# Attention and a gated feed-forward in one kernel: bfloat16 score corrections, v by a DMA transpose, weights ahead of the keys, one reciprocal per tile, a new order

## The chip, the cores and the metric

The kernel runs on one core of one Trainium2 chip. Its time is the device time of one execution, in microseconds (us), median of several runs. TensorE (PE in the profile) multiplies matrices, VectorE (DVE) and ScalarE (ACT) work on SBUF and PSUM, GpSimd (POOL) on SBUF alone, and SyncE (SP) issues every DMA of this kernel. Each engine works through its own list in order and waits on semaphores for the others.

## The reference

Four batches; q has 12288 rows of 128. The keys, which are also the values, are means of kv over windows of 4 x 4, 768 rows of 128 per batch, times a 128 x 128 matrix. The attention's output goes into a feed-forward with a squared ReLU and a sigmoid gate, in which each row is mixed with the row before it.

```python
kv_pool = kv.reshape(B, H // r, r, W // r, r, C).mean(axis=(2, 4))
k = v = kv_pool.reshape(B, -1, C) @ w_sr
s = (q @ k.transpose(0, 2, 1)) / np.sqrt(C)
a = np.exp(s - s.max(-1, keepdims=True))
a /= a.sum(-1, keepdims=True) + 1e-09
x = a @ v
x_prev = x shifted by one row
xk = mu_k * x + (1.0 - mu_k) * x_prev          # xr in the same way with mu_r
k = np.maximum(xk @ w_k, 0.0)                   # 128 -> 1024
out = 1.0 / (1.0 + np.exp(-(xr @ w_r))) * (k * k @ w_v)
```

Everything is float32. The kernel gets there with narrower products by splitting: an operand is rounded to a high part, the rest is a low part, and high x low, low x high and high x high are added in PSUM.

## The kernel before

The host hands over q transposed (`qT`), the kv windows with channels on partitions (`kv0` for the first batch, `kvw` for the others) and the three feed-forward weights as 64-bit words, two 32-bit halves each, which the kernel converts into pairs of 16-bit matrices (`wkh`, `wkl`, `wvh`, `wvl`, `wvb`, `wrh`, `wrl`).

**A tile** is 512 rows of q; there are 24 per batch, 96 in all. Its steps, with the names of the code:

- `qf` loads, `qh` (ScalarE) rounds to fp32r, `ql` (POOL) is the rest.
- `S0` to `S3`: the scores of 128 rows each against 768 keys, in chunks of 512 and 256 columns. A *score group* is the six products of one `S`: `ql` x `ksh`, `qh` x `ksl`, `qh` x `ksh` in each chunk, all fp32r.
- `nm` (VectorE): the negated row maximum. `ex` (ScalarE): the exponential, with the row sum in `sm`. Its result `pe` is in SBUF for three groups; the fourth, `S3`, is overwritten in PSUM and stays there.
- `rc` (VectorE): two tiny instructions, 1/(sum) for two groups at a time. `f1` (ScalarE): the normalised fp16 part of `pp`. `f2` (VectorE, `pp<-pe,rc,pp`): its fp16 rest.
- `tt`: one DMA transpose per group, of both parts, into `pT`.
- `AV0` to `AV5` (`px<-pT,v`): 18 products with the fp16 parts `v1`, `v2` of v. `xe`, `xk`, `xr`: the mixing; `xkh`, `xkl`, `xrh`, `xrl`: the split.
- `ha`, `hb` (`ph`): 24 products for the hidden layer in four quarters; `r`, `k2`, `kh`, `kl`: ReLU, square and split, spread over ScalarE, VectorE and POOL; `va`, `vb` (`pv`): 24 products back. `z` (`pz`): 3 products for the gate; `th`, `T1`, `E`, `E1`, `g`, `o`, and `so` stores.

**Buffers.** A `Ring` hands out its buffers in turn, so a step that takes one waits for the last reader of what was in it. Scores and `ph` share the ring `big` of three PSUM buffers; `px`, `pz` and the key preparation share `x`, which has one. Key loads have six (`kv`), `pT` two.

**Once and per batch.** For the first batch the keys come in twelve loads of 512 KB: eight (`kva`) for keys 0 to 511, multiplied straight away in fp32 (`pk`), and four (`kvb`) summed on VectorE first (`four`). The weights are loaded (`raw`) and converted into 16 bits in steps whose names begin with `w`: about nine VectorE instructions for each 512 columns, an absolute-sum product with `ones` (`cs`) and a maximum for a common scale. For the later batches twelve key loads with a VectorE sum each (`br`, `acc<-kvt`) are spread over twelve tiles, and about a tile's time later comes `PREP`: `pk`, `ks`, `am`, `ex`, the split `ksh`, `ksl`, and v: `ksv` scales, `pt0` and `pt1` transpose on PE in fp32, `v1*` and `v2*` copy and split. `dg` with `ones` (in `pt1`) spreads a maximum over partitions; `sv` and `uz` are scales.

**Order.** The code writes no loop order. Each step is put on a heap with a number and taken off in the order of the numbers:

```python
def plan_tile(i, b, t):
    if i < len(EARLY):            places, base = EARLY[i], 0.0
    elif i >= NTILES - len(LATE): places, base = LATE[...], i * PERIOD
    else:                         places, base = WHEN, i * PERIOD
    def at(name):
        def put(fn): plan.add(places[name] + base, name, fn, ("tile", i))
```

`WHEN` is for the middle, `EARLY` for the first tiles (six lists), `LATE` for the last four, `ONCE` for the steps before the first scores and the weights, `PREP` for later batches. The numbers set only who stands before whom in each engine's list. Every instruction is recorded under one line of a helper (L37), so in the profile tiles tell the steps apart.

Of the kernel before, what the change touches and what calls it, by code (L numbers as in the profile page):

```python
# [23 lines left out]
K_SHIFT = 23  # L24

# [46 lines left out]
def tile_kernel(ctx, tc, qT, kv0, kvw, w_sr, mu_k, mu_r, w_k, w_v, w_r, outT):  # L72
# [20 lines left out]
    ones = const.tile([P, P], F32, name="ones")  # L93
    nc.vector.memset(ones, 1.0)
    wsr = const.tile([P, C], F32, name="wsr")
    nc.sync.dma_start(out=wsr, in_=w_sr)
# [8 lines left out]
    mu = const.tile([P, 2], F32, name="mu")  # L105
    mix = const.tile([P, 4], F32, name="mix")
    mtop = const.tile([P, 2], F32, name="mtop")
    cz = const.tile([P, 3], F32, name="cz")
# [3 lines left out]
    for name, shape, dtype in (  # L112
        ("qf", [P, T], F32), ("qh", [P, T], F32R), ("ql", [P, T], F32R),
        ("pe", [P, K], F32), ("sm", [P, NSUB], F32), ("rc", [P, NSUB], F32), ("nm", [P, 1], F32),
        ("pp", [P, 2, K], F16), ("pT", [P, NSUB, 2 * NK, P], F16),
        ("xek", [P, T + 1], F32), ("xer", [P, T + 1], F32), ("xk", [P, T], F32), ("xr", [P, T], F32),
        ("xkh", [P, T], F16), ("xkl", [P, T], F16), ("xrh", [P, T], F16), ("xrl", [P, T], F16),
        ("E", [P, T], F32), ("th", [P, T], F32), ("o", [P, T], F32),
        ("rr", [P, 2 * T], F32), ("kk", [P, 2 * T], F32), ("kh", [P, 2 * T], F16),
        ("kl", [P, 2 * T], BF16), ("kv", [P, 1024], F32),  # L120
        ("ksh", [P, K], F32R), ("ksl", [P, K], F32R), ("v1", [P, NK, P], F16), ("v2", [P, NK, P], F16),
        ("s4", [P, 4], F32), ("uz", [P, 3], F32), ("sc", [P, 1], F32),
        ("ks", [P, K], F32), ("acc", [P, K], F32), ("dg", [P, 2, P], F32),
    ):
        rings[name] = Ring(sb, name, shape, dtype, BUFS.get(name, 2))
# [24 lines left out]
    @once("L_mu")  # L150
    def _():
        for i, src in enumerate((mu_k, mu_r)):
            sp.dma_start(out=mu[:, i:i + 1], in_=src.rearrange("(p o) -> p o", o=1))

# [16 lines left out]
    def weights(name, w, hi, lo, half, extra):  # L171
        st = {}
        n = w.shape[1]
        least = 897.0 if half else 896.0
        parts = [(c, min(n, c + 512)) for c in range(0, n, 512)]
        top, rest = {}, {}

        def part(i, c0, c1):
# [8 lines left out]
            @once(f"we_{key}")  # L187
            def _():
                st["e", i] = take("xk", name="e", dtype=I32)[:, :d]
                dve.tensor_scalar(  # L190
                    st["e", i], st["raw", i][:, :, 1], 20, 0x7FF,
                    op0=ALU.logical_shift_right, op1=ALU.bitwise_and,
                )
# [37 lines left out]
            def _():  # L231
                if "top" not in st:
                    st["top"] = take("kk", name="top")
                st["t", i] = st["top"][:, c0:c1]
                dve.tensor_tensor(
                    out=st["t", i].bitcast(I32), in0=st["m", i], in1=st["ei", i], op=ALU.bitwise_or
# [3 lines left out]
            def _():  # L240
                if "rest" not in st:
                    st["rest"] = take("rr", name="rest")
# [6 lines left out]
            def _():  # L249
                st["a", i] = take("o", name="wabs")[:, :d]  # L250
# [26 lines left out]
        for i, (c0, c1) in enumerate(parts):  # L277
# [20 lines left out]
            if extra is not None:  # L298
                @once(f"wb_{name}{i}")
# [20 lines left out]
    def first_keys(ks, ksh, ksl):  # L320
        st = {"a": 0, "b": 0}
        for i in range(WIN // 2):
            @once(f"L_a{i}")
            def _(i=i):
                st[f"a{i}"] = take("kv", name="kva", shape=[P, 2, 512])
                sp.dma_start(out=st[f"a{i}"], in_=kv0[:, 2 * i:2 * i + 2, 0:512])

            @once(f"pa{i}")
            def _(i=i):
                if st["a"] == 0:  # L330
                    st["pk"] = take("big", name="pk")
# [7 lines left out]
        for i in range(WIN // 4):  # L339
            @once(f"L_b{i}")  # L340
            def _(i=i):
                st[f"b{i}"] = take("kv", name="kvb", shape=[P, 4, K - 512])
                sp.dma_start(out=st[f"b{i}"], in_=kv0[:, 4 * i:4 * i + 4, 512:K])

            @once(f"ab{i}")
            def _(i=i):
                st[f"s{i}"] = take("xek", name="four", shape=[P, K - 512])
                dve.tensor_reduce(
                    out=st[f"s{i}"], in_=st[f"b{i}"].rearrange("p w k -> p k w"), axis=AX.X,
                    op=ALU.add,  # L350
                )

            @once(f"pb{i}")
            def _(i=i):
                if st["b"] == 0:
                    st["pk2"] = take("big", name="pk")
                pe.matmul(
                    st["pk2"][:, 0:K - 512], lhsT=wsr, rhs=st[f"s{i}"],
                    start=(st["b"] == 0), stop=(st["b"] == WIN // 4 - 1),
                )  # L360
                st["b"] += 1

        for n, (c0, c1) in enumerate(CHUNKS):
# [12 lines left out]
            def _(c0=c0, c1=c1):
                dve.tensor_tensor(
                    out=ksl[:, c0:c1], in0=ks[:, c0:c1], in1=ksh[:, c0:c1].bitcast(F32),
                    op=ALU.subtract,
                )  # L380

    def later_keys(b, i0, at, ks, ksh, ksl):
        st = {}

        def part(n):
# [30 lines left out]
        @at("ksh")  # L416
        def _():
            dve.tensor_copy(out=ksh, in_=ks)

        @at("ksl")  # L420
        def _():
            pool.tensor_tensor(out=ksl, in0=ks, in1=ksh.bitcast(F32), op=ALU.subtract)

    def batch_prep(b, i0, res):
# [10 lines left out]
        ks, ksh, ksl = take("ks"), take("ksh"), take("ksl")  # L435
        (later_keys if later else first_keys)(*((b, i0, at) if later else ()), ks, ksh, ksl)
        v1, v2, s4, uz, sc = (take(n) for n in ("v1", "v2", "s4", "uz", "sc"))
# [3 lines left out]
        res += [ksh, ksl, v1, v2, s4, uz, sc]  # L441
        st = {}
# [11 lines left out]

        @at("dg")
# [7 lines left out]
        @at("ksv")  # L463
        def _():
            st["ksv"] = take("acc", name="ksv")
            dve.tensor_scalar_mul(st["ksv"], ks, ivs)

        for h, (j0, j1) in enumerate(((0, 4), (4, NK))):
            @at(f"pt{h}")
            def _(h=h, j0=j0, j1=j1):  # L470
                pt = st["pt", h] = take("x", name="pt", shape=[P, 4, P])
# [30 lines left out]
        def _():  # L502
            dve.tensor_scalar_mul(uz, cz, xt[:, 1:2])
            dve.tensor_scalar(sc, cv, xt[:, 0:1], xt[:, 0:1], op0=ALU.mult, op1=ALU.mult)

    def plan_tile(i, b, t):
        st = {}
        if i < len(EARLY):
# [594 lines left out]
```

## Time and profile before

| | us |
|---|---|
| timed runs: median (lowest to highest) of 3 | 1919.85 (1918.26 to 1920.95) |
| profiled execution, span from first to last instruction | 1917.4 |
| what the median has beside that span | 2.45 |
| granted PE clock, mean | 0.995 |
| PE / VectorE / ScalarE / POOL busy | 1881.0 / 1754.2 / 1699.9 / 1069.0 |

In rows of groups the columns are: line, engine, operation, out<-in, shapes, count, then busy us and mean ns, then the idle time before and what ended it. An fp32 product is recorded as two. PE's records overlap, since products are pipelined: what one costs is the distance from its start to the next start, and not its length. A window row gives the stretch, then busy us and instructions of PE, weight loads (PEld), VectorE, ScalarE and POOL, then PE's clock, the busy share of the DMA engines and GB/s.

### The profile page before, as it was taken

The numbers are of one execution on the slowest core, as the hardware profiler recorded it, in microseconds if no ns is written. First come the engines' busy times: TensorE is split into PE (matmuls) and PEld (weight loads), VectorE is DVE, ScalarE is ACT, GpSimd is POOL, SyncE is SP. The second block draws the span as 40 slices with busy tenths as digits, with TensorE's granted clock in tenths as the row PEclk, the third lists the DMA queues.
The fourth block names the chain that finished last, engine by engine and source line by source line (L and its number), as shares of the span: only waits on it lengthen the run. The fifth ranks groups of instructions, "written<-read, shape, count | busy, mean of one in ns | idle before, by whom it ended". The sixth has DMA issues, their size and how long they took to land.

```text
span 1917.4 us, 26966 instructions
## 1 busy us (share of the span) xinstructions
PE 1881.0 (98%) x9022; PEld 1033.4 (54%) x9022; DVE 1754.2 (91%) x2582; ACT 1699.9 (89%) x2432; POOL 1069.0 (56%) x784
## 2 busy tenths in 40 slices
PE   7699999999999999999999999999999999999999
PEld 4355555555555555555555555555555555555554
DVE  5999999998999999999999999999898989898898
ACT  3699998899898989889999999988999999999997
POOL 1265555556565656556555555555555555555556
PEclk9899999999999999999999999999999999999999
DMA  6556564546566666446566656554646464655452
GB/s 224 117 127 141 135 146 97 105 108 116 116 141 136 139 136 130 99 104 117 103 140 130 146 132 144 111 110 97 124 97 124 97 124 96 124 98 123 83 118 59
DMA packets 640523, 230.57 MB, mean 120 GB/s; under 512 B 606336, under 2 KB 608640, under 8 KB 640384
## 3 DMA queue, kind: packets, MB, share of 16 engines
q1 hardware_dynamic: 640384, 228.85, 56.0%
q8 instruction: 71, 1.16, 0.3%
q14 instruction: 68, 0.56, 0.1%
HBM read 52.63 MB, written 25.17 MB: 41 GB/s over the span
## 4 chain that ended last, share of the span: by engine, by line
PE 94%; DVE 3%; ACT 1%; DMA 1%; issue 1%; SPq 0%; DVEq 0%
PE pv L37 26%; PE ph L37 25%; PE S L37 20%; PE px L37 19%; PE pz L37 3%; DVE pp L37 1%; DVE nm L37 1%; PE pk L37 0%; DMA kva<-kv 0%; DMA kvb<-kv 0%; ACT pp L37 0%; PE pt L37 0%; DVE top L37 0%; ACT rr L37 0%; SPq L37 0%
## 5 line engine op out<-in xcount | busy, mean ns | idle before, releaser
L37 POOL TENSOR_TENSOR kl<-kk,kh 128x1024 bf16<-128x1024 f32 x288 | 653.8, 2271 | 240.5 <-ACT kh L37 226.2
L37 ACT ACTIVATE rr<-ph 128x1024 f32<-128x1024 f32 x384 | 392.8, 1024 | 46.1 <-PE ph L37 40.1
L37 DVE TENSOR_REDUCE nm<-S 128x1 f32<-128x768 f32 x384 | 364.8, 952 | 66.4 <-PE S L37 59.3
L37 PE MATMUL px<-pT,v 128*128 128x512 f16 x1728 | 421.8, 380 | 3.3 <-DVE xr L37 2.9
L37 POOL TENSOR_TENSOR xrl<-xr,xrh 128x512 f16<-128x512 f32 x96 | 146.3, 1524 | 326.6 <-DVE xrh L37 326.6
L37 PE MATMUL S<-ksh,ql 128*128 128x512 f32 (+1 forms) x768 | 299.0, 389 | 8.9 <-ACT pe L37 4.7
L37 ACT ACTIVATE kh<-rr 128x1024 f16<-128x1024 f32 x288 | 302.7, 1052 | 2.3 <-PE pv L37 1.7
L37 DVE SCALAR_TENSOR_TENSOR pp<-pe,rc,pp 128x768 f16<-128x768 f32 x288 | 292.3, 1037 | 1.8 <-ACT pp L37 1.7
L37 PE MATMUL ph<-xkh,wkl 128*128 128x512 f16 x768 | 291.1, 379 | 2.2 <-ACT pe L37 2.2
L37 ACT ACTIVATE pp<-pe,rc 128x768 f16<-128x768 f32 x288 | 260.3, 938 | 36.5 <-DVE rc L37 32.1
L37 PE MATMUL pv<-kh,wvl 128*128 128x512 f16 x768 | 292.0, 380 | 0.0
L37 PE MATMUL pv<-kh,wvh 128*128 128x512 f16 x768 | 291.1, 379 | 0.0
L37 PE MATMUL ph<-xkh,wkh 128*128 128x512 f16 x768 | 291.1, 379 | 0.0
L37 PEld LDWEIGHTS <-v 128*128 128x128 f16 x1728 | 169.3, 98 | 209.2 <-issue 6.1
L37 DVE TENSOR_TENSOR kk<-ph,rr 128x1024 f32<-128x1024 f32 x192 | 234.7, 1223 | 48.6 <-ACT rr L37 48.5
L37 ACT ACTIVATE pe<-S,nm 128x768 f32<-128x768 f32 x288 | 258.7, 908 | 11.2 <-DVE nm L37 9.8
L37 PE MATMUL S<-ksl,qh 128*128 128x512 f32 (+1 forms) x768 | 260.9, 340 | 0.2 <-ACT ks L37 0.2
L37 PE MATMUL S<-ksh,qh 128*128 128x512 f32 (+1 forms) x768 | 260.9, 340 | 0.0
L37 PEld LDWEIGHTS <-wkh 128*128 128x128 f16 x1536 | 150.3, 98 | 183.6 <-issue 3.4
L37 PE MATMUL ph<-xkl,wkh 128*128 128x512 f16 x768 | 228.1, 379 | 0.0
L37 POOL TENSOR_TENSOR xkl<-xk,xkh 128x512 f16<-128x512 f32 x96 | 113.7, 1184 | 198.8 <-DVE rc L37 180.9
L37 PE MATMUL pv<-kl,wvb 128*128 128x512 bf16 x768 | 213.2, 379 | 0.0
(120 smaller groups left out, 2811.4 us busy)
## 6 DMA issues: line engine op xcount, KB each, us to landing
qf<-qT SPq DMA_DIRECT2D x96, 256.0 KB, 3.2
outT<-o SPq DMA_DIRECT2D x96, 256.0 KB, 3.0
kvt<-kvw SPq DMA_DIRECT2D x36, 512.0 KB, 4.6
pT<-pp SPq DMA_TRANSPOSE x384, 3.8
kva<-kv SPq DMA_DIRECT2D x8, 512.0 KB, 5.4
kvb<-kv SPq DMA_DIRECT2D x4, 512.0 KB, 6.4
raw<-moe_w_k SPq DMA_DIRECT2D x2, 512.0 KB, 7.0
raw<-moe_w_v SPq DMA_DIRECT2D x2, 512.0 KB, 7.3
```

The costliest lines, as they stand in the source:

```text
L37: return self.tc.keep_in_program_order(op(*args, **kwargs))
```

## The change

1. **Scores.** The two correction products of each chunk are bfloat16: `ql` is written as bfloat16, the keys get `kbl` (a bfloat16 copy and a bfloat16 rest), and the upper 16 bits of `qh` are read as bfloat16, every second element (`qb`). `qh` x `ksh` stays fp32r. All four corrections come first, then the two fp32r products.
2. **v.** `vh` (ScalarE) and `vl` (VectorE) make the fp16 parts with keys along the free axis, and `tv`, one DMA transpose per batch, makes `vT`. The PE transposes are gone; `dm` is the bfloat16 remainder of `pt1`.
3. **The head.** `w_sr` and the two `mu` come as one load (`head`). The weights land in the two `pT` buffers (`land`), which the first tiles don't need yet, instead of the key ring; their loads stand ahead of most of the key loads, and most of their conversion ahead of the keys' use. The conversion is written anew: six VectorE instructions of 512 columns up to `top` and `ei`, as before, from magnitude and sign. Keys 512 to 767 of the first batch are summed over all 16 window places at once (`acc<-kvb`), and one product follows.
4. **Reciprocal.** From tile 8 on, one `rc` pair per tile instead of two.
5. **Order.** New `WHEN`, `PREP`, `ONCE`, `EARLY` (now eight lists), `LATE`; the sums of later keys are one tile later.

```diff
-        ("qf", [P, T], F32), ("qh", [P, T], F32R), ("ql", [P, T], F32R),
+        ("qf", [P, T], F32), ("qh", [P, T], F32R), ("ql", [P, T], BF16),
...
+                qb = st["qh"].bitcast(BF16).rearrange("p (t h) -> p t h", h=2)[:, sl, 1]
+                for c0, c1 in CHUNKS[::-1]:
+                    pe.matmul(S[:, c0:c1], lhsT=ql, rhs=kbl[:, 0, c0:c1], start=True, stop=False)
+                    pe.matmul(S[:, c0:c1], lhsT=qb, rhs=kbl[:, 1, c0:c1], start=False, stop=False)
                 for c0, c1 in CHUNKS:
-                    o = S[:, c0:c1]
-                    pe.matmul(o, lhsT=ql, rhs=ksh[:, c0:c1], start=True, stop=False)
-                    pe.matmul(o, lhsT=qh, rhs=ksl[:, c0:c1], start=False, stop=False)
-                    pe.matmul(o, lhsT=qh, rhs=ksh[:, c0:c1], start=False, stop=True)
+                    pe.matmul(S[:, c0:c1], lhsT=qh, rhs=ksh[:, c0:c1], start=False, stop=True)
...
+            @at(f"kb{n}")
+                if later: pool.tensor_copy(out=put("kbl")[:, 0, c0:c1], in_=ks[:, c0:c1])
+                else: act.copy(out=put("kbl")[:, 0, c0:c1], in_=ks[:, c0:c1])
+            @at(f"kd{n}")
+                (pool if later else dve).tensor_tensor(out=put("kbl")[:, 1, c0:c1], in0=ks[:, c0:c1],
+                    in1=res["ksh"][:, c0:c1].bitcast(F32), op=ALU.subtract)
...
+        @at("vh")
+            act.activation(out=st["vv"][:, 0, :], in_=ks, func=AF.Copy, scale=ivs)
+        @at("vl")
+            dve.scalar_tensor_tensor(out=st["vv"][:, 1, :], in0=ks, scalar=ivs, in1=st["vv"][:, 0, :],
+                op0=ALU.mult, op1=ALU.subtract)
+        @at("tv")
+            sp.dma_start_transpose(out=put("vT"), in_=st["vv"].rearrange("p a k -> p (a k)"))
-            @at(f"pt{h}")
-                for j in range(j0, j1):
-                    pe.transpose(pt[:, j - j0, :], st["ksv"][:, j * P:(j + 1) * P], ident)
-                if h:
-                    pe.matmul(pt[:, 2:4, :], lhsT=ones, rhs=st["dg"], start=True, stop=True)
+        @at("dm")
+            pe.matmul(st["dm"], lhsT=ones, rhs=st["dg"], start=True, stop=True)
...
+    def landing(j, part, shape):
+            land[j] = take("pT", name="land", shape=[P, 3, 512, 2], dtype=I32)
-                st["raw", i] = take("kv", name="raw", shape=[P, d, 2], dtype=I32)
+                st["raw", i] = landing(*place[i], d)
...
+        group = {s: s | 1 if i < PAIRS else NSUB - 1 for s in range(NSUB)}
-            if s % 2 == 1:
+            if s in group.values():
                 @at(f"rc{s}")
-                    sm, rc = st[f"sm{s - 1}"][:, 0:2], new(f"rc{s - 1}")[:, 0:2]
+                    s0 = min(x for x in group if group[x] == s)
+                    sm, rc = st[f"sm{s}"][:, s0:s + 1], new(f"rc{s}")[:, s0:s + 1]
                     dve.tensor_scalar(rc, sm, 1e-9, 2.0 ** -15, op0=ALU.add, op1=ALU.mult)
                     dve.reciprocal(rc, rc)
...
+PAIRS = 8
 WHEN = {
-    ... "S0": 55.51, "S1": 56.462, ... "rc1": 63.617, "f10": 63.761, "S2": 64.341, ...
+    ... "S0": 104.19131, "S1": 104.19276, ... "S3": 111.47258, ... "rc3": 114.93419, "f10": 116.09149, ...
```

Where the order moves, at the places that matter below. PE, one score group in a middle tile; before:

```order
L37 MATMUL S<-ksh,ql 128x512
L37 MATMUL S<-ksl,qh 128x512
L37 MATMUL S<-ksh,qh 128x512
L37 MATMUL S<-ksh,ql 128x256
L37 MATMUL S<-ksl,qh 128x256
L37 MATMUL S<-ksh,qh 128x256
```

The same group now (an fp32r product loads its weights by itself, so the loads have rows only for 16-bit ones):

```order
L39 LDWEIGHTS ql
L39 MATMUL S<-kbl,ql 128x256
L39 LDWEIGHTS qh
L39 MATMUL S<-kbl,qh 128x256
L39 LDWEIGHTS ql
L39 MATMUL S<-kbl,ql 128x512
L39 LDWEIGHTS qh
L39 MATMUL S<-kbl,qh 128x512
L39 MATMUL S<-ksh,qh 128x512
L39 MATMUL S<-ksh,qh 128x256
```

The small chunk moves to the front for the corrections, and only two of six products read `ksh`.

SP, the loads of the head; before, from its second row on (`kva` and `kvb` are keys, `raw` are weights):

```order
L37 DMA kva<-kv 128x2x512
L37 DMA qf<-qT 128x512
L37 DMA kva<-kv 128x2x512
L37 DMA kvb<-kv 128x4x256
L37 DMA kva<-kv 128x2x512
L37 DMA kvb<-kv 128x4x256
L37 DMA kva<-kv 128x2x512
L37 DMA mu<-moe_mu_k 128x1
L37 DMA mu<-moe_mu_r 128x1
L37 DMA kva<-kv 128x2x512 x2
L37 DMA qf<-qT 128x512
```

and now (`land` are weights), up to the four loads of q:

```order
L39 DMA land<-moe_w_k 128x1024 x2
L39 DMA kvb<-kv0b 128x1024 x2
L39 DMA kva<-kv0a 128x1024
L39 DMA land<-moe_w_v 128x1024
L39 DMA land<-moe_w_r 128x256
L39 DMA kva<-kv0a 128x1024
L39 DMA land<-moe_w_v 128x1024
L39 DMA kva<-kv0a 128x1024 x5
L39 DMA kvb<-kv0b 128x1024 x2
L39 DMA kva<-kv0a 128x1024
L39 DMA qf<-qT 128x512 x4
```

All weights are issued before the last eight key loads, and the first q comes after all keys instead of third.

VectorE in the head, from the first maxima on; before (`ef`, `ei` and `m` belong to the weights):

```order
L37 TENSOR_REDUCE nm<-S 128x1
L37 TENSOR_SCALAR e<-raw 128x512
L37 TENSOR_SCALAR rc<-sm 128x2
L37 RECIPROCAL rc<-rc 128x2
L37 TENSOR_SCALAR ef<-e 128x512 x2
L37 SCALAR_TENSOR_TENSOR pp<-pe,rc,pp 128x768
L37 TENSOR_SCALAR ksv<-ks,ivs 128x768
L37 SCALAR_TENSOR_TENSOR pp<-S,rc,pp 128x768
L37 TENSOR_REDUCE nm<-S 128x1
L37 SCALAR_TENSOR_TENSOR pp<-pe,rc,pp 128x768
L37 TENSOR_SCALAR ei<-ef 128x512
L37 TENSOR_SCALAR m<-raw 128x512
```

and now, in the stretch before the keys are complete (`mag`, `sign`, `top`, `ei` belong to the weights, `acc<-kvb` to the keys):

```order
L39 TENSOR_SCALAR sign<-land 128x512
L39 TENSOR_REDUCE acc<-kvb 128x64 x2
L39 TENSOR_SCALAR mag<-mag 128x512 x2
L39 SCALAR_TENSOR_TENSOR top<-mag,sign 128x512
L39 TENSOR_SCALAR mag<-mag 128x512
L39 TENSOR_SCALAR mag<-land 128x512
L39 TENSOR_SCALAR mag<-mag 128x512
L39 TENSOR_SCALAR sign<-land 128x512
L39 TENSOR_SCALAR mag<-mag 128x512
L39 TENSOR_SCALAR ei<-top 128x512
```

The conversion stood among the softmax of the first tiles; now most of it stands before the first `nm`.

More of the change, by code (lines that the diff above doesn't have):

```diff
@@ L92, in tile_kernel @@
     make_identity(nc, ident)
-    ones = const.tile([P, P], F32, name="ones")
+    ones = const.tile([P, P], BF16, name="ones")
     nc.vector.memset(ones, 1.0)
-    wsr = const.tile([P, C], F32, name="wsr")
-    nc.sync.dma_start(out=wsr, in_=w_sr)
+    first = const.tile([P, C + 2], F32, name="first")
+    nc.sync.dma_start(out=first, in_=head)
+    wsr, mu = first[:, 0:C], first[:, C:C + 2]
     pe, act, dve, pool, sp = (
@@ L169, in _, with weights @@
         dve.tensor_scalar_max(mtop, mtop, 1.0)
-    def weights(name, w, hi, lo, half, extra):
+    land = {}
+    def landing(j, part, shape):
+        if j not in land:
+            land[j] = take("pT", name="land", shape=[P, 3, 512, 2], dtype=I32)
+        return land[j][:, part, :shape, :]
+    def weights(name, w, hi, lo, place, extra):
         st = {}
         n = w.shape[1]
-        least = 897.0 if half else 896.0
         parts = [(c, min(n, c + 512)) for c in range(0, n, 512)]
-        top, rest = {}, {}
         def part(i, c0, c1):
@@ L241, in _ @@
                 if "rest" not in st:
-                    st["rest"] = take("rr", name="rest")
+                    st["rest"] = take("rr", name="rest") if n > P else one(f"rest_{name}", n=n)
                 st["r", i] = st["rest"][:, c0:c1]
@@ L433, in at, with put @@
             return put
-        ks, ksh, ksl = take("ks"), take("ksh"), take("ksl")
-        (later_keys if later else first_keys)(*((b, i0, at) if later else ()), ks, ksh, ksl)
-        v1, v2, s4, uz, sc = (take(n) for n in ("v1", "v2", "s4", "uz", "sc"))
+        def put(key, name=None):
+            if key not in res:
+                res[key] = take(name or key)
+            return res[key]
+        st = {}
+        ks = take("ks")
+        later_keys(b, i0, at, ks) if later else first_keys(ks)
         ex, exs, ivs = (one(n) for n in ("ex", "exs", "ivs"))
@@ L440, in batch_prep, with _ @@
         exi = one("exi", I32)
-        res += [ksh, ksl, v1, v2, s4, uz, sc]
-        st = {}
+        for n, (c0, c1) in enumerate(CHUNKS):
+            @at(f"ksh{n}")
+            def _(c0=c0, c1=c1):
+                dve.tensor_copy(out=put("ksh")[:, c0:c1], in_=ks[:, c0:c1])
+            @at(f"kb{n}")
+            def _(c0=c0, c1=c1):
+                if later:
+                    pool.tensor_copy(out=put("kbl")[:, 0, c0:c1], in_=ks[:, c0:c1])
+                else:
+                    act.copy(out=put("kbl")[:, 0, c0:c1], in_=ks[:, c0:c1])
+            @at(f"kd{n}")
+            def _(c0=c0, c1=c1):
+                (pool if later else dve).tensor_tensor(
+                    out=put("kbl")[:, 1, c0:c1], in0=ks[:, c0:c1],
+                    in1=res["ksh"][:, c0:c1].bitcast(F32), op=ALU.subtract,
+                )
         @at("am")
@@ L544, in _ @@
             def _(s=s):
-                ksh, ksl = bps[b][:2]
+                ksh, kbl = bps[b]["ksh"], bps[b]["kbl"]
                 S = st[f"S{s}"] = take("big", name="S")
@@ L562, in _ @@
             def _(s=s):
[L563 to L564 removed]
+                if f"sm{group[s]}" not in st:
+                    new(f"sm{group[s]}")
                 if PE_AT[s] == "P":
@@ L796, in tile_kernel @@
     seq = [(b, t) for b in range(B) for t in range(NT)]
-    bps = {b: [] for b in range(B)}
+    bps = {b: {} for b in range(B)}
     batch_prep(0, 0, bps[0])
-    weights("wk", w_k, wkh, wkl, False, None)
-    weights("wv", w_v, wvh, wvl, False, wvb)
-    weights("wr", w_r, wrh, wrl, False, None)
+    weights("wk", w_k, wkh, wkl, ((0, 0), (0, 1)), None)
+    weights("wv", w_v, wvh, wvl, ((0, 2), (1, 0)), wvb)
+    weights("wr", w_r, wrh, wrl, ((1, 1),), None)
     for i, (b, t) in enumerate(seq):
```

298 lines of the change are left out of this document (132 added, 166 removed), and 430 rows, old and new, of tables (EARLY, LATE, ONCE, PREP).

## The prediction

> **What bounds the kernel now.** I read the busy line of the page, then windows over the stages, then the chain of waits, then TensorE's (PE's) timeline.
>
> ```profile
> PE 1881.0 (98%) x9022; PEld 1033.4 (54%) x9022; DVE 1754.2 (91%) x2582; ACT 1699.9 (89%) x2432; POOL 1069.0 (56%) x784
> ```
>
> Three engines are near full, so averages decide nothing. By stretch (PE, weight loads, VectorE, ScalarE, GpSimd; clock; DMA):
>
> ```profile
> 0.00:24.00 24.00, 17.60 (x36) 7.41 (x37) 6.75 (x13) 2.52 (x3) 3.27 (x9) 1.00 0.89 305
> 0.00:100.00 100.00, 69.98 (x237) 40.04 (x238) 76.67 (x157) 50.96 (x87) 19.61 (x27) 0.90 0.63 170
> 30.00:90.00 60.00, 39.85 (x146) 25.96 (x145) 55.45 (x123) 38.65 (x70) 11.82 (x12) 0.83 0.52 111
> 213.64:309.23 95.59, 95.59 (x466) 52.73 (x465) 90.98 (x131) 87.78 (x126) 55.72 (x41) 1.00 0.61 128
> 309.23:408.51 99.28, 98.36 (x479) 54.25 (x477) 92.40 (x144) 89.18 (x129) 56.52 (x42) 1.00 0.52 107
> 408.51:523.26 114.75, 114.75 (x559) 63.23 (x558) 103.87 (x151) 105.10 (x150) 66.35 (x49) 1.00 0.57 115
> 1880.00:1917.40 37.40, 33.81 (x157) 15.13 (x155) 28.10 (x35) 26.15 (x31) 24.43 (x15) 1.00 0.19 50
> ```
>
> In the middle PE never idles (95.59 of 95.59) while VectorE is at 95% with key sums and 91% without: PE is the bound. From 30 to 90 us PE is under 70% and VectorE at 92%: the head is VectorE's. Around 365 us, where the batch changes, 0.92 us of PE is lost. The chain of waits cut at the same ten `pv` products of each tile:
>
> ```profile
> 213.64 2.16 PE pv L37 x10
> ...
> 219.90 2.59 PE px L37 x12
> ...
> 232.77 2.16 PE pv L37 x10
> ```
>
> The cut recurs after 19.13 us, and the window from 213.64 to 309.23 is five such: 19.12 us a tile. A 512-column 16-bit product takes 2.59/12 = 0.216. A tile has 69 of these (18 `px`, 24 `ph`, 24 `pv`, 3 `pz`), 14.89 us; the remaining 4.23 are four score groups of 1.058. So 96 tiles need 96 x 19.12 = 1835.5. What PE had done by 100 us:
>
> ```profile
> L37 PE MATMUL S<-ksh,ql 128*128 128x512 f32 (+1 forms) x36 | 16.5, 458 | 8.9 <-ACT pe L37 4.7 <-DVE pp L37 4.1
> L37 PE MATMUL px<-pT,v 128*128 128x512 f16 x50 | 13.1, 420 | 3.3 <-DVE xr L37 2.9 <-DVE mx_wr L37 0.4
> L37 PE MATMUL ph<-xkh,wkh 128*128 128x512 f16 x6 | 2.3, 378 | 0.0
> ```
>
> 18 score groups (36 products, two chunks each), 50 `px`, 18 `ph` (three rows of six), 3 `pz`: 19.0 + 10.8 + 3.9 + 0.6 = 34.4 us of tile work, so the head loses 65.6. Each batch change costs 99.28 - 5 x 19.12 = 3.68. Together 65.6 + 1835.5 + 11.0 = 1912.1 of the span's 1917.4; the last 5.3 are the end (3.6 of PE idle and the last store). The timed runs' median, 1919.85, lies 2.45 above this span; I keep that offset.
>
> **Scores in bfloat16.** Four of six products of a group change from fp32r to bfloat16.
>
> ```profile
> 809.86 0.40 PE L37 MATMUL S<-ksh,ql 128*128 128x512 f32 x1
> 810.09 0.40 PE L37 MATMUL S<-ksl,qh 128*128 128x512 f32 x1
> 810.33 0.40 PE L37 MATMUL S<-ksh,qh 128*128 128x512 f32 x1
> 810.57 0.28 PE L37 MATMUL S<-ksh,ql 128*128 128x256 f32 x1
> 810.69 0.28 PE L37 MATMUL S<-ksl,qh 128*128 128x256 f32 x1
> 810.81 0.28 PE L37 MATMUL S<-ksh,qh 128*128 128x256 f32 x1
> ```
>
> Starts are 0.23 to 0.24 apart for 512 columns and 0.12 for 256, against 0.216 in 16 bits and 0.108 for half of that. A group at the 16-bit rate would be 4.5 x 0.216 = 0.971, so six fp32r products cost 0.087 too much, 0.0145 each. Four of them mended: 0.058 a group, 0.232 a tile, a tile of 18.89. 372 groups lie where PE is the bound (384 less the 12 of the new head): -21.6. No row shows a 16-bit load of weights with a stride, which `qb`, the upper halves of `qh`, needs:
>
> ```profile
> L37 PEld LDWEIGHTS <-wvb 128*128 128x128 bf16 x768 | 74.7, 98 | 89.5
> L37 PEld LDWEIGHTS S<-ksl,qh 128*128 128x128 f32 x768 | 146.2, 190 | 23.7 <-issue 0.9 <-ACT ks L37 0.5 <-DVE ksl L37 0.3
> ```
>
> If such a load behaves like the 190 ns row, its products keep the fp32r rate and only the `ql` pair gains: -10.8. If it behaves like the 98 ns row, all of it: I take that, being 16-bit too. The Trainium skill (TensorE: Matmul & The Clock Gate, section Weight-path perf modes) says that fast loading is on for 128 weights of any type but FP32, with column steps up to 1,024 elements; the 98 and 190 ns agree for dense loads, and by that rule the term stays -21.6. POOL's `ql` writes half the bytes, on an engine at 56%; 0.
>
> **Does the middle stay PE's?** VectorE loses one of two reciprocal pairs a tile (this row and its reciprocal, as long):
>
> ```profile
> L37 DVE TENSOR_SCALAR rc<-sm 128x2 f32<-128x2 f32 x192 | 32.3, 168 | 4.9 <-ACT S L37 0.7
> ```
>
> So 90.98 / 5 = 18.20 becomes 17.86 against 18.89, 95%, as now; ScalarE has 105.10 / 6 = 17.52, 93%. Nothing else becomes the bound by its sum, and the reciprocal itself brings PE nothing. All four normalisations now wait for the fourth exponential; that is rival B.
>
> **Batch change.** Out go the fp32 transposes of v and their wait:
>
> ```profile
> 365.22 0.66 PE L37 MATMUL pt<-ident,ksv 128*128 128x128 f32 x4 [0.92 <-DVE xr L37]
> 365.71 0.38 PE L37 MATMUL pv<-kh,wvl 128*128 128x512 f16 x1
> ...
> 371.49 0.38 PE L37 MATMUL pt<-ident,ksv 128*128 128x128 f32 x2
> ...
> 372.14 0.38 PE L37 MATMUL ph<-xkh,wkl 128*128 128x512 f16 x1
> ```
>
> 0.92 + 0.49 + 0.65 = 2.06; `dm` in bfloat16 puts 0.11 back: -1.95 three times, -5.9. The DMA transpose stands on SP between `pT` transposes, and what is behind it waits until `vl` is done on VectorE. PE would pay when that exceeds the slack of `AV`: 0 to 3.8 each (landing of the row below); I take 0, since `vl` comes before in the order. The `kb` and `kd` steps on POOL replace one subtraction per batch: covered by POOL's 44% idle, and wanted only by the next batch's first scores, more than a tile away in the order.
>
> ```profile
> pT<-pp SPq DMA_TRANSPOSE x384, 3.8
> ```
>
> **The head.** Five weight loads (2.23 MB) move on SP's queue ahead of most of the 6.29 MB of keys, q behind them; with `head` 8.59 MB land before the last key. At the 305 GB/s of the first 24 us that is 28.2 us, against a last key now at 23.78:
>
> ```profile
> 23.78 1.90 DVE L37 TENSOR_REDUCE four<-kvb 128x256 f32<-128x1024 f32 x1 [0.93 <-DMA kvb<-kv]
> 28.75 1.81 DVE L37 TENSOR_REDUCE nm<-S 128x1 f32<-128x768 f32 x2
> ...
> 86.37 0.42 DVE L37 CAST xkh<-xk 128x512 f16<-128x512 f32 x1
> ```
>
> The first row maximum (`nm`) then starts at 28.2 + (28.75 - 23.78) = 33.2, 4.4 later: this part costs. In return most of the weights' conversion moves into the wait for the keys, in which VectorE is busy 6.75 of 24 us. Before, 58.0 us pass from the first `nm` to the `xkh` that lets `ph` start. In the new order VectorE has to do between these two 11 `nm`, 8 `pp`, and, worked from the same rows and shorter ones, 9.7 us of others (`vl` 1.04, two `dg`, five reciprocal pairs 1.7, two `wd` and two `wo` 3.0, `ei` 0.6, `xk`, `xkh` and scalars 2.7):
>
> ```profile
> L37 DVE TENSOR_REDUCE nm<-S 128x1 f32<-128x768 f32 x384 | 364.8, 952 | 66.4 <-PE S L37 59.3
> L37 DVE SCALAR_TENSOR_TENSOR pp<-pe,rc,pp 128x768 f16<-128x768 f32 x288 | 292.3, 1037 | 1.8 <-ACT pp L37 1.7
> L37 DVE SCALAR_TENSOR_TENSOR wkl<-rest,gain_wk,top 128x512 f16<-128x512 f32 x2 | 1.5, 743 | 0.0
> ```
>
> 10.5 + 8.3 + 9.7 = 28.5, at the 92.4% of the window from 30 to 90: 30.8. `ph` starts at 64.0. By then PE has done 12 groups and 18 `px`, 12.0 + 3.9 = 15.9: loss 48.1. About 4 us of conversion are left for VectorE after it, and PE has a backlog of one tile of softmax less than before; I add 3.5. 51.6 against 65.6: -14.0. Ends: VectorE without a gap and no loss after it gives `ph` at 61.7, -20; the old 58.0 us again from 33.2 gives a loss of 75.3, +9.7. I take the middle way since the removed work is counted and VectorE is what the head waits for.
>
> **The end.** The order has 106 products after the last `px` where it had 90, so less of the last tile's chain lies open: between 0 and the 3.6 idle, and as much loss if the new order fails; -1.
>
> **Sum:** 1919.85 - 21.6 - 5.9 - 14.0 - 1.0 = 1877.
>
> **Rivals.**
> A, the strided load isn't fast: the S term is -10.8, 1888. For it: no such row exists. Against it: the 98 ns of both 16-bit types.
> B, the other side: one reciprocal makes scores hold PSUM longer. `S3` stays in one of three big buffers until its `pp` correction ends, and the `ha2` of the next tile takes that buffer. If the chain `S3`, `nm`, exponential, reciprocal, `pp`, correction ends late, PE waits there once a tile, and behind `ha2` everything queued on PE. From 42.5/96 = 0.44 us a tile on the change is no faster; at 0.5 it is 1925. For it: ScalarE already waits for the reciprocal, and it will wait for the last of four exponentials instead of two:
>
> ```profile
> ACT pp L37 <- DVE rc L37: 32.6, 77, 1.4
> ```
>
> Against it: these 32.6 us reach PE nowhere in the middle, in a chain of the same links.
> C, weights ahead of keys only delay: the head ends as in its bad end, 1901. For it: 4.4 us are sure. Against it: VectorE's 92%.
>
> **How the numbers follow.** Forecast as worked 0.70; A 0.15; C 0.10 (0.02 of it with enough else to end level); B 0.05, 0.01 of it level. Faster by over 0.2% (about what a measurement of this kernel tells from no change) 0.70 + 0.15 + 0.08 = 0.93, same 0.03, slower 0.04. Upwards the range takes in A and half of C, 1898, and leaves out B; downwards it reaches by the head's good end (6), the end's (3) and some faster landing of the keys to 1865. The likeliest case alone: 1865 to 1888.
>
> **What would show it.** Right: score groups 1.00 apart, a tile 18.9 in a quiet stretch, loads of `qh` for `kbl` near 98 ns; no PE idle at batch changes; the first `nm` near 33, the first `ph` near 64. Wrong: PE idle before `ph` or `S` in every tile (B), loads of 190 (A), `ph` after 75 (C).

## The result, and the profile after

| | before | after |
|---|---|---|
| timed runs, median (lowest to highest), us | 1919.34 (1918.26 to 1920.95) | 1902.26 (1902.06 to 1903.22) |
| profiled span, us | 1917.4 | 1900.3 |

The ratio is 0.9912, with a 95% interval of 0.9898 to 0.9926: faster by 17 us. The forecast was 1877, in a range of 1865 to 1898. The sign was right, but the gain was 17 us where 42 had been worked out. The busy line of the page after:

```profile
PE 1844.3 (97%) x8837; PEld 925.9 (49%) x8983; DVE 1750.9 (92%) x2400; ACT 1690.0 (89%) x2430; POOL 1110.4 (58%) x793
```

PE is busy for 37 us less, and a point less of the span (a part of that is records missing from the trace: of 768 `pv<-kl,wvb` it has 673). VectorE has 182 instructions fewer, but only 3 us less of busy time. That mismatch is the first hint: some instructions of VectorE have become longer.

**The quiet tiles.** The start of the same 18 `px` products, nine tiles apart in the timeline after; then, in the kernel before, the start of the same 12, sixteen tiles apart:

```profile
480.70 4.05 PE L39 MATMUL px<-pT,vT 128*128 128x512 f16 x18
...
651.29 4.05 PE L39 MATMUL px<-pT,vT 128*128 128x512 f16 x18
```

```profile
452.84 2.75 PE L37 MATMUL px<-pT,v 128*128 128x512 f16 x12
...
759.07 2.75 PE L37 MATMUL px<-pT,v 128*128 128x512 f16 x12
```

170.59 / 9 = 18.954 us a tile after, 306.23 / 16 = 19.139 before: 0.185 less, where 0.232 was forecast; 17.8 us over 96 tiles. Here the change does what it was meant to do.

**The batch change.** The same `px` eight tiles apart, around a change of batch, and PE's own waits between them (start, duration, engine, instruction, then the idle time before it and what ended it):

```profile
765.01 4.05 PE L39 MATMUL px<-pT,vT 128*128 128x512 f16 x18
...
813.58 0.38 PE L39 MATMUL ph<-xkh,wkl 128*128 128x512 f16 x1 [1.14 <-ACT rr L39]
...
817.05 0.27 PE L39 MATMUL S<-kbl,ql 128*128 128x256 bf16 x1 [0.29 <-ACT pe L39]
...
849.66 0.39 PE L39 MATMUL ph<-xkh,wkl 128*128 128x512 f16 x1 [0.77 <-DVE pp L39]
...
854.01 0.38 PE L39 MATMUL ph<-xkh,wkl 128*128 128x512 f16 x1 [0.87 <-ACT rr L39]
...
922.04 4.05 PE L39 MATMUL px<-pT,vT 128*128 128x512 f16 x18
```

157.03 - 8 x 18.954 = 5.40 us for a change of batch, where it was 3.68. The wait for `xr` and the fp32 transposes are gone, and four other waits are there, 3.07 us in the rows. Followed back, two VectorE instructions stand at their root. VectorE, GpSimd and ScalarE at these moments:

```profile
809.38 0.15 DVE L39 TENSOR_SCALAR exs<-exi 128x1 f32<-128x1 f32 x1
...
809.65 1.58 DVE L39 CAST ksh<-ks 128x256 fp32r<-128x256 f32 x1
811.16 0.74 DVE L39 SCALAR_TENSOR_TENSOR xr<-px,s,xer 128x512 f32<-128x512 f32 x1
...
845.79 2.89 DVE L39 SCALAR_TENSOR_TENSOR vv<-ks,ivs,vv 128x768 f16<-128x768 f32 x1
848.60 1.00 DVE L39 SCALAR_TENSOR_TENSOR pp<-S,rc,pp 128x768 f16<-128x768 f32 x1
```

```profile
808.60 2.49 POOL L39 TENSOR_TENSOR kl<-kk,kh 128x1024 bf16<-128x1024 f32 x1 [0.49 <-ACT kh L39]
...
845.67 2.18 POOL L39 TENSOR_TENSOR kl<-kk,kh 128x1024 bf16<-128x1024 f32 x1 [1.22 <-ACT kh L39]
```

```profile
811.93 0.69 ACT L39 ACTIVATE xek<-px,s 128x512 f32<-128x512 f32 x1 [2.83 <-DVE xr L39]
```

A cast of 256 columns takes 1.58 us, and the rest of v (`vl`, the row `vv<-ks,ivs,vv`) 2.89, where the same form `pp<-pe,rc,pp` takes 1.0. Each of the two starts while a GpSimd `kl` is running and ends by about its own usual length after that `kl` ends: 845.67 + 2.18 = 847.85, and 845.79 + 2.89 - 1.01 = 847.67. Behind the cast stands `xr`, behind `xr` ScalarE's `xek` and `rr`, and PE's `ph` waits for that `rr`. Behind `vl` stands the correction of `S3`, which holds the PSUM buffer of the next `ph`: this is the wait that rival B named, at three places and not in every tile.

**The head.** The first row maximum and the first `ph` came early, as far as the working went (33.2 and 64.0 were forecast):

```profile
32.53 0.94 DVE L39 TENSOR_REDUCE nm<-S 128x1 f32<-128x768 f32 x1
```

```profile
60.12 0.41 PE L39 MATMUL ph<-xkh,wkl 128*128 128x512 f16 x1 [1.35 <-DVE xkh L39]
```

What PE had done by 229 us, from the groups of that window (44 score groups of two fp32r products each, 162 `px`, 3 x 68 `ph`, 3 x 64 `pv`, 3 x 8 `pz`):

```profile
L39 PE MATMUL px<-pT,vT 128*128 128x512 f16 x162 | 38.9, 379 | 2.3 <-DMA pT<-pp 2.2
L39 PE MATMUL S<-ksh,qh 128*128 128x512 f32 x88 | 31.8, 443 | 0.0
L39 PE MATMUL ph<-xkh,wkl 128*128 128x512 f16 x68 | 27.2, 399 | 6.3 <-DVE pp L39 3.2 <-DVE xkh L39 1.3 <-DVE kk L39 1.2
L39 PE MATMUL pv<-kh,wvl 128*128 128x512 f16 x64 | 24.4, 380 | 0.1
L39 PE MATMUL pz<-xrh,wrl 128*128 128x512 f16 x8 | 3.0, 380 | 0.0
```

A quiet tile leaves (18.954 - 69 x 0.2158)/4 = 1.015 us for a score group. 44 x 1.015 + 582 x 0.2158 = 170.3 us of tile work in 229: the head loses 58.7, against 65.6 before and 51.6 in the forecast. The same count at 100 us gives 52.2, so the forecast held up to there; 6.5 us more are lost between 100 and 229 us, where the kernel before loses nothing. That stretch, before and after (PE, weight loads, VectorE, ScalarE, GpSimd):

```profile
100.00:229.07 129.07, 129.07 (x625) 69.67 (x624) 122.54 (x167) 117.21 (x165) 81.05 (x56) 1.00 0.59 135
```

```profile
100.00:229.07 129.07, 123.97 (x592) 61.63 (x602) 124.53 (x166) 111.87 (x161) 70.54 (x51) 0.99 0.59 131
```

VectorE is busy longer with one instruction fewer, and PE idles for 5.1 us. The granted clock is not the reason: it is 0.50 from 97.9 to 101.3 us and 1.00 from there to 229, which costs this stretch 0.7 us at most. Four of VectorE's instructions of the head, and GpSimd at the second:

```profile
46.85 1.24 DVE L39 TENSOR_SCALAR rc<-sm 128x2 f32<-128x2 f32 x1
...
91.85 2.89 DVE L39 SCALAR_TENSOR_TENSOR pp<-pe,rc,pp 128x768 f16<-128x768 f32 x1
...
146.34 2.09 DVE L39 TENSOR_SCALAR rc<-sm 128x2 f32<-128x2 f32 x1
...
192.55 2.71 DVE L39 SCALAR_TENSOR_TENSOR pp<-pe,rc,pp 128x768 f16<-128x768 f32 x1
```

```profile
91.74 2.19 POOL L39 TENSOR_TENSOR kl<-kk,kh 128x1024 bf16<-128x1024 f32 x1 [3.29 <-DVE kk L39]
```

Fifteen of VectorE's instructions in the first 200 us exceed the shortest of their form by more than 0.2 us, 19.1 us in all; before there are seven with 3.4 us. At the start of each of the fifteen a GpSimd instruction was running, and each ended by its own shortest length, less 0.1 to 0.2 us, after that instruction's end.

**Which forms wait.** The view of a tile gives the shortest, median and longest duration of a form over the whole run (ns):

```profile
L39 DVE TENSOR_REDUCE nm<-S x384: 936/956/959, 32.5 to 1852.0; 128x1 f32<-128x768 f32 x192
L39 DVE TENSOR_TENSOR kk<-ph,rr x192: 1206/1211/1225, 67.6 to 1885.6; 128x1024 f32<-128x1024 f32 x192
L39 DVE SCALAR_TENSOR_TENSOR pp<-S,rc,pp x96: 1003/1008/1019, 41.2 to 1856.7; 128x768 f16<-128x768 f32 x96
L39 DVE RECIPROCAL rc<-rc x104: 165/178/179, 36.0 to 1854.3; 128x4 f32<-128x4 f32 x88, 128x2 f32<-128x2 f32 x16
L39 DVE SCALAR_TENSOR_TENSOR pp<-pe,rc,pp x288: 997/1007/2894, 39.4 to 1864.0; 128x768 f16<-128x768 f32 x144
L39 DVE TENSOR_SCALAR rc<-sm x104: 154/169/2091, 35.8 to 1854.1; 128x4 f32<-128x4 f32 x88, 128x2 f32<-128x2 f32 x16
L39 DVE CAST ksh<-ks x8: 275/501/1584, 28.1 to 1321.7; 128x256 fp32r<-128x256 f32 x4, 128x512 fp32r<-128x512 f32 x4
```

The first three read PSUM, and never vary by more than 23 ns; the reciprocal, in SBUF alone, varies by 14. The last three have all their inputs in SBUF, and go up to twelve times their median. So theory P: a VectorE instruction of such a form waits until the GpSimd instruction that is running has ended, and the profile counts the wait as busy. The Trainium skill (SBUF — State Buffer, section Who interferes with whom) has a rule for such waits: VectorE's second port pair is GpSimd's only one, an exclusive lock; copies, casts, `tensor_scalar` and instructions with two SBUF inputs can contend, `tensor_reduce` and instructions with one SBUF input outside the two-port modes don't, and the one that issues second waits for the whole of the other. The rows agree. The prediction did not use it.

The kernel before has such waits too, only fewer: one `pp` at each change of batch took 2.93 us, the longest of its row:

```profile
L37 DVE SCALAR_TENSOR_TENSOR pp<-pe,rc,pp x288: 999/1009/2934, 35.4 to 1883.0; 128x768 f16<-128x768 f32 x144
```

So this view of the kernel before would have shown the wait ahead of the forecast.

The rival, theory W: there is simply too much VectorE work in the new head and at the batch change, wherever it stands.

### The profile page after: what moved, and what is told of

It reads as the page before. It is cut to its first block, busy times and chain, and to the rows that moved or that the text cites. A ratio compares the mean times of both kernels' runs of the same rounds, so it can differ in the third digit from the quotient of the medians.

```text
span 1900.3 us, 26528 instructions
## 1 busy us (share of the span) xinstructions
PE 1844.3 (97%) x8837; PEld 925.9 (49%) x8983; DVE 1750.9 (92%) x2400; ACT 1690.0 (89%) x2430; POOL 1110.4 (58%) x793
## 5 line engine op out<-in xcount | busy, mean ns | idle before, releaser
L39 POOL TENSOR_TENSOR kl<-kk,kh 128x1024 bf16<-128x1024 f32 x288 | 685.3, 2380 | 182.4 <-ACT kh L39 119.9
L39 PE MATMUL px<-pT,vT 128*128 128x512 f16 x1728 | 391.9, 379 | 2.3 <-DMA pT<-pp 2.2
L39 POOL TENSOR_TENSOR xkl<-xk,xkh 128x512 f16<-128x512 f32 x96 | 145.3, 1514 | 320.8 <-DVE xkh L39 318.1
L39 DVE SCALAR_TENSOR_TENSOR pp<-pe,rc,pp 128x768 f16<-128x768 f32 x288 | 300.3, 1045 | 0.0
L39 PE MATMUL S<-ksh,qh 128*128 128x512 f32 (+1 forms) x768 | 269.4, 432 | 0.0
L39 PEld LDWEIGHTS <-vT 128*128 128x128 f16 x1728 | 168.7, 98 | 206.1 <-issue 3.6
L39 PE MATMUL S<-kbl,qh 128*128 128x256 bf16 (+1 forms) x768 | 251.2, 327 | 2.7
L39 POOL TENSOR_TENSOR xrl<-xr,xrh 128x512 f16<-128x512 f32 x96 | 113.5, 1183 | 239.0 <-DVE xrh L39 239.0
L39 PEld LDWEIGHTS <-wkh 128*128 128x128 f16 x1536 | 150.6, 98 | 180.3 <-issue 12.6
L39 PE MATMUL S<-kbl,ql 128*128 128x256 bf16 (+1 forms) x717 | 215.1, 325 | 14.3 <-DVE pp L39 5.3
L39 PE MATMUL pv<-kl,wvb 128*128 128x512 bf16 x673 | 187.1, 379 | 4.7
```

Source lines behind the costliest of these rows:

```text
L39: return self.tc.keep_in_program_order(op(*args, **kwargs))
```

## The experiments

Ratios are to the kernel before, run on the same chip, with 95% intervals. The median of the kernel before was 1919.3 to 1920.1 beside these runs, so a difference of 1 us between two rows says nothing.

| run | median us | ratio |
|---|---|---|
| e1_moved | 1891.88 | 0.9854 (0.984 to 0.9867) |
| e2_pool_light | 1888.96 | 0.9839 (0.9826 to 0.9853) |
| e3_s_undone | 1919.99 | 1.0001 (0.9992 to 1.001) |
| e4_two_rc | 1906.66 | 0.9929 (0.9916 to 0.9941) |
| e5_by_column | 1899.71 | 0.9894 (0.9877 to 0.991) |
| e6_both | 1890.93 | 0.9849 (0.9834 to 0.9864) |
| e7_moved_light | 1878.28 | 0.9789 (0.9775 to 0.9802) |
| e8_before_light | 1919.19 | 0.9997 (0.9988 to 1.0005) |
| e9_better | 1890.37 | 0.9851 (0.9836 to 0.9866) |

**e1_moved: two instructions elsewhere.**

```diff
 PREP = {
-    ... "ksh1": 83.51417, ... "vl": 121.214, ...
+    ... "ksh1": 84.5, ... "vl": 114.6, ...
```

> The changed kernel, with two VectorE instructions of each later batch's preparation at other places in VectorE's order: `ksh1` (256 columns of the key cast) one instruction later, behind `xr`, and `vl` (the rest of v) seven instructions earlier, ahead of `rc`. Both new places are moments at which GpSimd was idle in the trace. Theory P (a VectorE instruction with its inputs in SBUF waits until the GpSimd instruction that is running ends): `ksh1` falls from 1.58 to about 0.3 us and `vl` from 2.89 to about 1.0, and the PE idle before `ph` and `S` that follows them (1.41 + 0.45 and 0.93 + 1.14 us at the change seen) mostly goes; three changes of batch give back 8 to 12 us: 1890 to 1894. Theory W (the preparation is simply too much work for VectorE and ScalarE, wherever it stands): the stalls stay, 1901 to 1903.

1891.88, 10.4 us less than the changed kernel. `vl` and `ksh` over the run, and the eight tiles around the same change of batch:

```profile
L39 DVE SCALAR_TENSOR_TENSOR vv<-ks,ivs,vv x4: 1009/1010/1012, 37.1 to 1293.5; 128x768 f16<-128x768 f32 x4
```

```profile
L39 DVE CAST ksh<-ks x8: 275/481/922, 28.3 to 1311.7; 128x256 fp32r<-128x256 f32 x4, 128x512 fp32r<-128x512 f32 x4
```

```profile
761.96 4.05 PE L39 MATMUL px<-pT,vT 128*128 128x512 f16 x18
...
915.52 4.05 PE L39 MATMUL px<-pT,vT 128*128 128x512 f16 x18
```

153.56 - 8 x 18.954 = 1.93: the change of batch costs 3.47 less, three times 10.4, which is the whole gain, and PE's records show no idle time in these tiles. The same instructions with the same inputs stand in the same tiles: theory W falls here. `ksh1` still took 0.92, so it met the end of a `kl`, but `xr` now stands ahead of it. So e1 does two things at once: it shortens the waits, and it takes the two instructions out of the way of `xr` and of the correction of `S3`. No run separates these; the waits alone, 1.58 - 0.28 and 2.89 - 1.01, come to 3.2 of the 3.47 us.

**e2_pool_light: less for GpSimd in the head.** `ql`, `xkl`, `xrl` and GpSimd's `kl` of the first eight tiles keep 64 columns; the other columns of these low parts are left out, and their buffers are filled with zeros once at the start:

```diff
+        def cut(n):
+            return slice(0, 64 if i < 8 else n)
-                    out=new(f"x{x}l"), in0=st[f"x{x}"], in1=st[f"x{x}h"], op=ALU.subtract
+                    out=new(f"x{x}l")[:, cut(T)], in0=st[f"x{x}"][:, cut(T)],
+                    in1=st[f"x{x}h"][:, cut(T)], op=ALU.subtract
```

> The changed kernel, with GpSimd's work in the first eight tiles cut to 64 columns of 512 or 1024 (`ql`, `xkl`, `xrl`, `kl`: the low parts are left out in the other columns, so the first eight tiles are less exact); VectorE, ScalarE and PE have the same instructions in the same order. Theory P: of the 17 us that VectorE instructions of the first 200 us take beyond their shortest time, some 13 go, and PE's loss in the head falls from 58.7 to 48 to 54 us: 1891 to 1898. Theory W (the head is long because of the amount of VectorE's work): VectorE stays at 98% from 50 to 200 us and the time stays within 2 us of 1902.

1888.96, 13.3 less. The `px` that started at 229.07 after, in the same place of the order, here and there:

```profile
229.07 4.05 PE L39 MATMUL px<-pT,vT 128*128 128x512 f16 x18
```

```profile
216.62 4.05 PE L39 MATMUL px<-pT,vT 128*128 128x512 f16 x18
```

```profile
100.00:229.07 129.07, 128.88 (x633) 64.56 (x632) 122.24 (x169) 117.31 (x168) 29.52 (x53) 1.00 0.63 137
```

12.45 of the 13.3 us are won by then. In the stretch where PE had idled, it is busy for 128.88 of 129.07, and VectorE does three instructions more in 2.3 us less. Its waits in the first 200 us fall from 19.1 to 3.7. A rival reading is that the low parts simply reach PE sooner. Against it: in the changed kernel no wait of PE between 30 and 229 us was ended by GpSimd; the largest sums were ended by VectorE's `pp` (5.3 us before `S`, 3.2 before `ph`) and ScalarE's `pe` (3.4).

**e8_before_light: the control.** The same cut in the kernel before.

> A control: the kernel before, with GpSimd's low parts of the first eight tiles cut in the same way. In its trace VectorE's instructions of the first 200 us waited 3.4 us, not 17. Theory P: at most those 3.4 us and what the shorter way of the low parts to PE saves come back: 1914 to 1919. If less work for GpSimd speeds up any head, by shortening the chain to PE, the gain is like that of the changed kernel, 10 or more: 1906 to 1910, and the 13.3 us say nothing on the change.

1919.19, within 1 us of the kernel before. Less work for GpSimd is no gain by itself; it is one in the order in which VectorE's SBUF instructions meet GpSimd's. The control covers the first 100 us alone, since PE is busy all the time from 100 to 229 us in the kernel before.

**e7_moved_light: both together.**

> The changed kernel with both: `ksh1` and `vl` at the places where GpSimd is idle, and GpSimd's low parts of the first eight tiles cut to 64 columns (the rest of those low parts is left out). If the waits for GpSimd are the whole of what the prediction missed, the two gains add: 1902.3 - 10.4 - 13.3 = 1878.6, within 3 of the 1877 that was predicted. If both only shift one and the same limit: 1886 to 1889.

1878.28, where 1878.6 was the sum: the two losses are separate and add, and nothing of them is hidden behind the other.

**e3_s_undone: the scores alone.**

```diff
-("ql", [P, T], BF16) ... ("kbl", [P, 2, K], BF16)
+("ql", [P, T], F32R) ... ("kbl", [P, 2, K], F32R)
-                qb = st["qh"].bitcast(BF16).rearrange("p (t h) -> p t h", h=2)[:, sl, 1]
+                qb = qh
```

> The changed kernel with the score corrections in fp32r again (`ql`, both parts of `kbl`, and `qh` itself as weights), everything else and the order as it is. By the prediction's term, 0.232 us a tile, the time rises by 21.6 to 1924; by the period of the quiet tiles after (18.945 against 19.12), 0.175 to 0.185 a tile, by 17 to 18 to 1919 to 1920. If the order alone had made the middle faster, less than 5: 1907.

1919.99, the time of the kernel before. The scores are worth 17.7 us, and all the rest of the change together is worth nothing.

**e4_two_rc: two reciprocals again.** `PAIRS = 96`, and an `rc1` right ahead of each `rc3`.

> The changed kernel with two reciprocal pairs in every tile (rows 0 and 1, rows 2 and 3), standing one behind the other where the one pair stood. By the prediction the number of reciprocals is worth nothing, since VectorE waits about 0.4 us for the last exponential at that place: 1901 to 1904. If VectorE's work were what the middle waits for, 0.33 us in 88 tiles would come back: 1915 to 1931.

1906.66, 4.4 more than the changed kernel: outside both expectations, nearer to the first. Stretches of tiles of 19.01 us alternate with stretches of 18.95 in the middle. PE's overlapping records show no idle time in them, but the distances place the 0.06: the `ph` behind a tile's second score group starts 0.19 to 0.20 after the group's last product, where 0.12 is usual, and 0.05 after the end of ScalarE's `rr` (642.80 + 1.02 = 643.82, `ph` at 643.87). In the tiles of 18.95 this `rr` ends 0.3 us or more ahead. So the added pair delays the chain that frees the PSUM buffer of this `ph`. In the profiled executions that and the changes of batch are 2.9 of the 5.0 us; the rest stands in the head, 1.7 of it already at the first `px`, and stays open. The prediction put the reciprocal at nothing; it is worth a little.

**e5_by_column and e6_both: another form in the place of another order.**

```diff
-                    dve.tensor_scalar(rc, sm, 1e-9, 2.0 ** -15, op0=ALU.add, op1=ALU.mult)
+                    for c in range(s + 1 - s0) if i < PAIRS else (slice(None),):
+                        c = slice(c, c + 1) if i < PAIRS else c
+                        dve.tensor_scalar(
+                            rc[:, c], sm[:, c], 1e-9, 2.0 ** -15, op0=ALU.add, op1=ALU.mult
+                        )
```

In the first eight tiles `rc` is written one column at a time, and so is `uz` of the first batch (e6 has the places of e1 beside that).

> The changed kernel with the places as they are, and with two small VectorE instructions of the first eight tiles and the first batch written as one instruction for each column: the 128x2 TENSOR_SCALAR of `rc` (16 of them) and that of `uz`. In the changed kernel's trace six of these waited 0.97 to 1.94 us each, 7.9 us in all before 150 us, while TENSOR_SCALARs of 128x1 took 0.14 to 0.15 us even beside GpSimd (13 of them). Theory P with the addition that the 128x1 form does not wait for GpSimd: VectorE has 17 instructions more, some 2 us, and still gains 5 to 6 us in the head, of which PE's loss takes over part, since other instructions then meet GpSimd: 1896 to 1900. Theory W: more instructions, 1902 to 1904.

1899.71, 2.5 us less with 17 instructions more. None of the single-column instructions waited, as none of the 128x1 ones had (the row at 809.38 runs inside a `kl`). In the profiled execution, 1.3 us shorter than that of the changed kernel, the head loss falls by those 1.3, while VectorE's waits of the first 200 us fall from 19.1 to 12.6: not every wait of VectorE reaches PE. Two steps of the weights that had run free now met GpSimd (1.02 and 0.58 us).

> The two changed places of `ksh1` and `vl` together with the `rc` and `uz` of the head written by columns. Theory P: the gains lie in different stages and add, 10.4 us from the places and 2 to 6 from the columns: 1886 to 1890, faster than both kernels. If the gain of the columns is taken up by other collisions: 1891 to 1893.

1890.93: of the columns' 2.5 us, 1.0 is left beside the new places, within what these runs can tell apart, and outside the first expectation.

**e9_better: nothing left out.** e6 with four steps of the preparation at further places:

```diff
-    ... "ksh1": 84.5, ... "kd0": 141.02329, ... "kb0": 163.27481, "kd1": 163.27779,
+    ... "ksh1": 85.2, ... "kd0": 147.0, ... "kb0": 166.0, "kd1": 166.1,
```

> No work left out: the columns in the head, `vl` ahead of `rc`, `ksh1` behind `xk` (behind `xr` it still took 0.92 us), and three GpSimd steps of the preparation, `kd0`, `kb0` and `kd1`, ahead of the next `xkl`, where VectorE reads PSUM. Theory P: `rc` or `th`, `pp` and `E` after a change no longer wait (1.08 + 0.39 + 0.30 us in the version with both moves), up to 0.7 us of PE a change: 1888 to 1891, against 1890.9.

1890.37. `ksh1` now takes 0.29 us, and of the waits after a change only 0.31 us of `E` is left. PE gains next to nothing by it, 0.09 us in one tile after a change: VectorE's slack had already covered the waits. It is faster than both kernels, by 1.5% and 0.6%; e1, e6 and e9 are equal within their spread.

## Why the prediction was wrong

| term | forecast | measured |
|---|---|---|
| scores | -21.6 | -17.7 (e3) |
| batch changes | -5.9 | +5.2 = 3 x (5.40 - 3.68) |
| head | -14.0 | -6.9 = 58.7 - 65.6 |
| end | -1.0 | +2.2 = 5.8 - 3.6 |
| sum | -42.5 | -17.2 (the runs: -17.1) |

**Batch change: the step that failed.** It counted what PE loses (the wait for `xr`, the transposes), and put the new `vl` and the cast at its new place at nothing ("I take 0, since `vl` comes before in the order"), as if VectorE's slack covered them. Their price is 1.01 and 0.28 us only while GpSimd is idle; they cost 2.89 and 1.58, and PE waits behind both. With that out of the way (e1) a change costs 1.93, 1.75 less than before: the -1.95 was right for what it counted. The slack of `AV`, which the step bounded, was never touched: behind the head no `px` waits for a DMA.

**Head: the step "I add 3.5".** First `nm` and first `ph` came at or ahead of the forecast, so the sum of VectorE's work was good, and the loss at 100 us was what the prediction gave for the end. The 3.5 for all that follows had no row behind it; it was 58.7 - 44 = 15 us, since the loss stood at 44 when `ph` started. The prediction took 92% as VectorE's efficiency, from a head in which it hardly meets GpSimd. In the new order it waits 19.1 us in the first 200. With GpSimd out of the way, the same order loses about 46 us instead of 58.7 (e2), less than the forecast. Rival C is out: the weights ahead of the keys put the first `nm` 3.8 us later, near the 4.4 counted, and the first `ph` still came 30 us earlier (60.12, where it was 90.28; the prediction took the end of `xkh` at 86.8 for it, but it stood behind the `px` products). That rival C's 1901 lies near the measured 1902 is chance. From 30 to 90 us the granted clock is 0.94, where it was 0.83; how much of the head's gain that is, no run separates.

**Scores: mechanism right, size off by 3.9.** Loads with a stride are as fast as dense ones (rival A is out), in the groups after:

```profile
L39 PEld LDWEIGHTS <-qh 128*128 128x128 bf16 x768 | 75.6, 98 | 46.8 <-issue 10.3
```

The groups are 1.00 to 1.01 apart, as forecast, but the product behind a group costs 0.23 too:

```profile
487.74 0.28 PE L39 MATMUL S<-kbl,ql 128*128 128x256 bf16 x1
...
488.75 0.39 PE L39 MATMUL ph<-xkh,wkl 128*128 128x512 f16 x1
488.98 0.38 PE L39 MATMUL ph<-xkh,wkh 128*128 128x512 f16 x1
489.20 0.38 PE L39 MATMUL ph<-xkh,wkl 128*128 128x512 f16 x1
```

The step spread the 0.087 over six products and left out this one, about 0.01 too long. In the new order the four groups of a tile stand in three places and not two, so it is paid three times. That and up to a hundredth in each group account for most of the 0.06 between 18.89 and 18.954.

**End.** PE's idle time in the last 100.3 us is 4.7 + 1.1 where it was 3.6, worked out from the rows below and the prediction's last window row: the forecast's bad end. VectorE waits for GpSimd there too (8.0 us from 1800 on, against 4.2); no run shows how much of it reaches PE.

```profile
1800.00:1862.90 62.90, 61.76 (x297) 30.61 (x301) 59.55 (x72) 56.45 (x80) 32.63 (x23) 1.00 0.54 109
1862.90:1900.30 37.40, 32.73 (x149) 14.65 (x150) 27.91 (x36) 25.54 (x30) 25.13 (x15) 1.00 0.19 50
```

```profile
1817.10:1880.00 62.90, 62.90 (x307) 34.23 (x305) 58.46 (x81) 58.16 (x82) 36.44 (x28) 1.00 0.50 105
```

**What held.** PE bounds the middle; rival B's wait is in no quiet tile. That 1878.28 (e7) is near 1877 is partly luck: there the head is better than forecast by most of what scores and end are worse. The range failed because its upper end added rivals that each touch one term, and no rival covered what two engines do to each other in all stages.

## What to carry to other kernels

Before you charge a moved or new VectorE instruction at its mean duration, look at what GpSimd runs at that moment: if its form is one of those that waited here (a cast, a `tensor_scalar` of more than one column, a `scalar_tensor_tensor` with SBUF inputs alone) and GpSimd is busy, add the rest of GpSimd's instruction, and then ask who waits behind it on VectorE. The view with shortest, median and longest duration of a form finds such waits in a minute, since they hide in busy time and no view of waits names them. In an order written by hand or by a planner, put VectorE's PSUM reads and reductions beside GpSimd's work, and the forms that wait into GpSimd's pauses.

## What the runs showed of the hardware that was not expected

- One column makes the difference: `rc` with 128x2 operands took up to 2.09 us beside GpSimd, the same one column at a time 0.14 to 0.15 inside a running GpSimd instruction (e5).
- SBUF operands alone do not make an instruction wait: the reciprocal `ivs<-exs` at 809.57 took 0.16 us inside the `kl` of 808.60, and 30 of the 36 reductions `acc<-kvt` of the kernel before (all 1.204 to 1.216) ran wholly inside a GpSimd instruction.
- It works in both directions: GpSimd's `kl` beside a VectorE instruction took 2.49 us (808.60, started while a `pp<-pe,rc,pp` of 808.09 to 809.09 was running) where 2.18 (845.67) is usual.
- A 16-bit product behind fp32r ones costs 0.23 instead of 0.216 us. By that, grouping the fp32r products would save about 0.01 us for each place less; no run tried it.
